# Masked attention with a rational FFN on one core: the planner's DMA reckoning, fillers for TensorE, and the products with V in two steps

## The chip, the cores and the metric

The kernel runs on one core of a Trainium2 chip. The core has four engines that compute (PE, the matrix engine, with its weight loads shown apart as PEld; DVE, the vector engine; ACT, the scalar engine; POOL) and SP, which here only issues DMAs. Each engine works through its own list of instructions in the written order and waits on semaphores where an instruction needs another engine's result. The metric is device time in microseconds (us), lower is better.

## What is computed

Eight batches of eight heads, 576 positions, 64 values per head. The attention keeps only scores within tau of the row's maximum; the heads' outputs side by side are the rows x of a feed-forward network with a rational activation.

```python
def _attn_ref(q, k, v, tau) -> np.ndarray:
    scale = 1.0 / np.sqrt(q.shape[-1])
    scores = scale * np.matmul(q, k.transpose(0, 1, 3, 2))
    thresh = np.max(scores, axis=-1, keepdims=True) - tau
    scores = np.where(scores >= thresh, scores, -1000000000.0)
    scores = scores - np.max(scores, axis=-1, keepdims=True)
    attn = np.exp(scores)
    attn = attn / (np.sum(attn, axis=-1, keepdims=True) + 1e-09)
    return np.matmul(attn, v).astype(np.float32)
...
    h = x @ w_in
    h2 = h * h
    h3 = h2 * h
    P = a[0] + a[1] * h + a[2] * h2 + a[3] * h3
    Q = 1.0 + np.abs(b[0]) * np.abs(h) + np.abs(b[1]) * h2
    g = P / (Q + 1e-06)
    return (g @ w_out).astype(np.float32)
```

x has 4608 rows of 512, w_in is 512 x 2048, w_out 2048 x 512, all in float32.

## The kernel before

**Precision.** A float32 factor is carried as two float16 parts, a rounded part ("hi") and a remainder ("lo"), and a product of two such factors is three float16 products: hi by hi, lo by hi, hi by lo. This holds for both FFN products and, after the first batch, for probabilities times V. In the first batch (PLAIN) that product runs in float32 and the transposes are made by TensorE.

**Attention.** The work is cut into units: a pair of heads and a tile of 128 queries (four full tiles and a rest of 64). For a unit PE multiplies queries and keys (lines 915, 922, 926), DVE takes the row maxima (932), ACT applies threshold and exponential (947, 951) into a buffer e, ACT or DVE writes the rounded part to a buffer hi (through the helper at 381) and DVE the remainder back over e (973). SP then issues two transposing DMAs (983), pT from hi and pT from e, and for two units together PE multiplies with V (1044): 30 matmuls of a 64-column array tiling, two heads side by side, five chunks c of the keys, three products each. ACT and DVE copy the result to x as two parts (1054, 1060).

**FFN.** A step takes 256 rows of x and 8 blocks of w_in: PE (1289), then a chain of ACT and DVE operations on tiles t (1299 to 1354), then PE with w_out (1363). ACT or DVE scales the result (1371, 1377), and it is stored (1386, 1390).

**Loads.** The weights come first, on POOL's DMA queue, each 1 MB load waiting on an earlier one (565). Q and K (755 to 766) and V (799, 803) of a pair come when their buffers (two, two and five) are free; from the ninth pair on they are on POOL's queue, while transposes and the copies of V's rounded part (863) are on SP's. POOL also computes the FFN's gains (1171 to 1217).

**Who sets the order.** Nothing in it is left to run time. A planner (class Plan) holds every operation with its engine (or a choice of engines, FLEX), its assumed duration, its dependencies and the buffers and PSUM banks that it takes and drops, and a key, which is its due time: a position in the sequence of units plus a constant for its kind (K) plus a shift of its unit or FFN step (SHIFT_UNITS, SHIFT_STEPS). order() simulates the engines: again and again it takes the operation that can start first and, among those within a tolerance (TOL), the one with the lowest key; the code is then emitted in that order. A DMA is a further engine of this simulation, "DMA" for SP's queue and "GD" for POOL's: it holds its queue for its duration, and its result counts as there a fixed LAT later (2.5 us on SP's queue, 3.3 on POOL's), no matter what else is under way. A transpose is given TPD, 1.3 us. Up to 120 us of planned time (LOADS_END) there are special rules: a load on POOL's queue is followed by a pause (PACED), a copy on SP's queue lasts twice as long plus 1 us, and a load on it lands 2 us later (LATE). A change of the array's tiling costs PE some 0.1 us in the plan (TURN), but doesn't enter the choice between operations while LAM is 0. Where PE has a pause in the plan, f_warm puts matmuls of an identity by itself into a free bank (1527) for 60% of the pause, before 400 us alone:

```python
            if e == "PE" and self.warm is not None and t < WARM_END:
                n = int((t - free[e]) * WARM / 0.22)
```

PSUM has eight banks. Scores of the first SINGLE units use either of two sets of three (0 to 2, 3 to 5), those of later units 0 to 2 alone; sums over w_out use one of 3 to 5, the first FFN product one of 5 and 6 (BH), and products with V, transposes on PE and small sums one of 7, 6 and 5 (B1).

Of the kernel before, what the change touches and what calls it, by code (L numbers as in the profile page):

```python
# [32 lines left out]
ENDK, ENDS = 2.59, 37.189  # L33

WHEN = [(-0.4, 1.998), (4.745, 1.263), (9.569, -0.366), (13.179, -0.311)]

V0, V1 = -1.222, -6.236

SINGLE = 22
# [35 lines left out]
AHEAD_RANK = 3.164  # L75

AHEAD = (1,) * 5 + (2,) * 11
PACED = (3.4, 0.5)
# [11 lines left out]
K = {"f1": 2.538, "f2": -0.829, "f4": -0.987, "f6": -1.195, "load": -5.828, "junk": 1.648, "sq": 1.739, "cn": -3.045,  # L90
     "cs": 0.032, "s1": -0.568, "s2": -5.401, "wh": 4.797, "wl": 1.319, "wc": 0.864, "vl": 0.529, "vc": 1.068, "vh": 1.802,
     "qk": -0.548, "max": -1.889, "thr": -0.221, "pre": -1.075, "sum": 2.999, "rec": 1.092, "rec2": 0.121, "diag": -0.725,
# [4 lines left out]

SHIFT_STEPS = {0: -0.894, 1: 3.213, 2: 0.769, 3: 3.605, 4: 1.271, 5: -0.037, 6: 1.022, 7: -0.168, 8: -1.488, 9: 2.739, 10: 0.4,
# [3 lines left out]

SHIFT_UNITS = {0: -1.177, 1: -0.45, 2: -1.342, 3: -1.061, 4: -1.427, 5: -0.333, 6: -0.175, 7: -0.27, 8: -2.113, 9: 0.228,
# [17 lines left out]

SHIFT_OPS = {}

LAM = 0.0

START = {"ACT": 4.777, "DVE": 4.281}
START_END = 104.113
EARLY = {"ACT": 1.482, "DVE": 4.089}
EARLY_END = 2093.721
PRICE = {"ACT": 10.914, "DVE": 0.624}  # L130

TOL = {"PE": 0.224, "ACT": 0.001, "DVE": 0.109, "POOL": 0.1, "DMA": 0, "GD": 0}
WARM, WARM_END = 0.6, 400.0

LOADS_END = 120.0

# [26 lines left out]
class Plan:  # L163
# [39 lines left out]
    def paced(self, e, o, t):  # L203
        if e != "GD" or not o.take or t >= LOADS_END:
            return 0.0
# [1364 lines left out]
```

## Time and profile before

| what | value |
|---|---|
| device time, median of 3 runs | 1319.86 us (1318.55 to 1327.18) |
| the profiled execution's own time | 1316.94 us |
| its span, first to last instruction | 1315.2 us |
| mean granted clock of TensorE | 0.979 |
| chain that ended last, by engine | PE 23%, ACT 14%, DVE 14%, DMA 8%, issue 4% |
| longest line of that chain | PE L1363 9%, DMA pT<-e 8%, PE L1289 6% |

How to read the rows: an instruction is named by its line (L1044), its engine, its operation, and what it writes and reads (pT<-e: the transpose that writes pT from e). "x30" counts instructions. Times behind an arrow are idle time of the engine, and the name behind the arrow is what ended it. A wait's row has the total in us, the number of waits and the longest. SPq and POOLq are the sequencers that issue DMAs. The granted clock is the share of TensorE's full clock.

### The profile page before, as it was taken

To read this page: it belongs to the slowest core of one execution; us is meant where nothing else is said; L and a number is where in the kernel's file an instruction comes from. 1 tells how busy PE (TensorE), PEld (TensorE's weight loads), DVE (VectorE), ACT (ScalarE), POOL (GpSimd) and SP (SyncE) were. 2 spreads that over 40 slices of the span, in tenths; PEclk is the share of its full clock that TensorE was granted. 3 is DMA by queue.
4 is the path that set the end of the run, shared out by engine and by line. 5 is a ranking of instruction groups with operands and counts; after the bars stand their busy time and mean duration, and the time that the engine had idled before them with its cause. 6 is when DMAs were issued, how large, how long until landed. Compare 5 with 4: busy or idle time off the path is not lost.

```text
span 1315.2 us, 25492 instructions
## 1 busy us (share of the span) xinstructions
PE 1222.9 (93%) x9444; PEld 786.3 (60%) x9444; DVE 1191.3 (91%) x1697; ACT 1142.1 (87%) x2165; POOL 392.3 (30%) x678
## 2 busy tenths in 40 slices
PE   7888899999998889999999799999999999999996
PEld 5556666675664646656656466675656665675652
DVE  6999999999997979999999689999989989999766
ACT  6999999998997979999998689999989888995643
POOL 2220240423142511552046241352315353400121
PEclk9999999999998989999999899999999999999998
DMA  8572285678557675586555684677547557650200
GB/s 226 201 236 84 87 156 98 120 163 171 92 116 115 136 109 102 105 163 130 92 113 96 103 160 97 136 147 150 90 88 151 122 133 140 123 97 18 53 16 16
DMA packets 344172, 156.30 MB, mean 119 GB/s; under 512 B 315136, under 2 KB 325104, under 8 KB 344048
## 3 DMA queue, kind: packets, MB, share of 16 engines
q1 hardware_dynamic: 321424, 93.83, 39.7%
q0 software_dynamic: 22304, 60.25, 17.0%
q8 instruction: 75, 1.23, 0.4%
q10 hardware_dynamic: 320, 0.59, 0.2%
q14 instruction: 49, 0.40, 0.1%
HBM read 63.25 MB, written 9.44 MB: 55 GB/s over the span
## 4 chain that ended last, share of the span: by engine, by line
PE 23%; ACT 14%; DVE 14%; DMA 8%; issue 4%; POOL 2%; POOLq 0%; ACTq 0%; DVEq 0%
PE banks L1363 9%; DMA pT<-e 8%; PE banks L1289 6%; PE banks L1044 4%; ACT e L947 3%; PE banks L926 3%; ACT e L951 2%; DVE e L973 2%; ACT hi L381 2%; DVE st L932 2%; DVE t L1354 2%; DVE t L1318 1%; ACT t L381 1%; DVE t L1328 1%; ACT t L1321 1%
## 5 line engine op out<-in xcount | busy, mean ns | idle before, releaser
L1363 PE MATMUL banks<-wp,t 128*128 128x512 f16 x1728 | 404.7, 383 | 11.1 <-ACT t L381 6.4
L1289 PEld LDWEIGHTS <-wi 128*128 128x128 f16 x3456 | 332.6, 98 | 97.6 <-issue 45.9
L1289 PE MATMUL banks<-x,wi 128*128 128x256 f16 x3072 | 364.1, 274 | 2.7 <-ACT t L1299 2.4
L1363 PEld LDWEIGHTS <-t 128*128 128x128 f16 x1728 | 164.0, 99 | 225.9 <-issue 45.6
L947 ACT ACTIVATE e<-banks,st 128x576 f32<-128x576 f32 x288 | 210.1, 740 | 27.2 <-DMA pT<-e 15.5
L951 ACT ACTIVATE e<-e,cf 128x576 f32<-128x576 f32 x288 | 223.1, 781 | 0.1
L973 DVE SCALAR_TENSOR_TENSOR e<-e,st,hi 128x576 f16<-128x576 f32 x252 | 201.9, 810 | 8.8 <-ACT hi L381 7.7
L932 DVE TENSOR_REDUCE st<-banks 128x2 f32<-128x1152 f32 x128 | 172.7, 1349 | 19.9 <-PE banks L926 14.2
L381 ACT ACTIVATE hi<-e,st 128x576 f16<-128x576 f32 x220 | 168.5, 774 | 5.6 <-DVE st L962 3.3
L1044 PE MATMUL banks<-pT,V 128*64 128x256 f16 (+1 forms) x2520 | 129.3, 254 | 35.8 <-DMA pT<-e 24.6
L1044 PEld LDWEIGHTS <-V 128*64 128x64 f16 x2520 | 107.7, 113 | 69.4 <-issue 50.8
L926 PE MATMUL banks<-KK,QQ 64*128 64x512 f32 x512 | 146.9, 651 | 0.0
L1299 ACT ACTIVATE t<-banks,hsc 128x512 f32<-128x512 f32 (+1 forms) x192 | 109.9, 586 | 21.0 <-PE banks L1289 17.4
L755 POOL DMA_DIRECT2D QQ<-in_qT_dram x47 | 25.2, 536 | 341.2 <-PE banks L915 193.1
L1354 DVE SCALAR_TENSOR_TENSOR t<-t,gsc,t 128x1024 f16<-128x1024 f32 (+2 forms) x69 | 90.7, 1323 | 12.0 <-ACT t L381 11.8
L1321 ACT ACTIVATE t<-t,co 128x1024 f32<-128x1024 f32 (+2 forms) x69 | 82.0, 1188 | 19.4 <-DVE t L1328 12.5
L1332 DVE SCALAR_TENSOR_TENSOR t<-t,co,t 128x1024 f32<-128x1024 f32 (+2 forms) x69 | 91.3, 1323 | 7.0 <-ACT t L1324 6.8
L1314 DVE SCALAR_TENSOR_TENSOR t<-t,co 128x1024 f32<-128x1024 f32 (+2 forms) x69 | 91.3, 1323 | 6.1 <-ACT t L1299 6.1
L381 ACT ACTIVATE t<-t,gsc 128x1024 f16<-128x1024 f32 (+1 forms) x66 | 78.1, 1197 | 18.2 <-DVE t L1340 12.7
L1340 DVE SCALAR_TENSOR_TENSOR t<-t,co,t 128x1024 f32<-128x1024 f32 (+2 forms) x69 | 91.2, 1322 | 0.1
L1328 DVE SCALAR_TENSOR_TENSOR t<-t,co,t 128x1024 f32<-128x1024 f32 (+2 forms) x69 | 91.2, 1322 | 0.0
L1318 DVE SCALAR_TENSOR_TENSOR t<-t,co 128x1024 f32<-128x1024 f32 (+2 forms) x69 | 91.1, 1322 | 0.0
(184 smaller groups left out, 1666.3 us busy)
## 6 DMA issues: line engine op xcount, KB each, us to landing
KK<-in_kT_dram POOLq DMA_DIRECT2D x94, 144.0 KB, 3.5
t<-in_w_in_dram POOLq DMA_DIRECT2D x8, 1024.0 KB, 7.2
t<-in_w_out_dram POOLq DMA_DIRECT2D x8, 1024.0 KB, 5.8
QQ<-in_qT_dram POOLq DMA_DIRECT2D x47, 144.0 KB, 3.0
V<-in_v_dram POOLq DMA_DIRECT2D x24, 256.0 KB, 4.0
out_dram<-u POOLq DMA_DIRECT2D x24, 256.0 KB, 3.8
QQ<-in_qT_dram POOLq DMA_DIRECT2D x47, 128.0 KB, 3.9
V<-u SPq DMA_DIRECT2D x28, 160.0 KB, 2.5
```

Of the source, the lines that this page charges most:

```text
L381: nc.scalar.activation(dst, src, AF.Identity, scale=factor)
L926: nc.tensor.matmul(d, QQ[r, t * P:(t + 1) * P], KK[r, REM:S], **one)
L932: nc.vector.tensor_reduce(box["st"][:, 0:2], box["both"], AX.X, ALU.max, negate=True)
L947: nc.scalar.activation(ev(hh), box["s"][hh], AF.Prelu, scale=SCALE, bias=box["st"][:, 2 + hh:3 + hh], alpha=STEEP)
L951: nc.scalar.activation(e, e, AF.Exp, scale=passes, accum_out=box["st"][:, 4 + hh:5 + hh])
L973: nc.vector.scalar_tensor_tensor(box["lo"][:, c], ev(hh), box["st"][:, 6 + hh:7 + hh], box["hi"][:, c], ALU.mult, ALU.subtract)
L1044: nc.tensor.matmul(dst, V[:, c * P + head * D:c * P + (head + 1) * D], rhs, start=c == 0 and n == 0, stop=c == NT and n == 2)
L1289: nc.tensor.matmul(d, wi_tile(c, f0 + j, hl), x[:, c, :], start=c == 0 and n == 0, stop=c == NC - 1 and n == 2)
L1299: nc.scalar.activation(box["h3"][:, 2 * k:2 * k + 2, sl], psv[:, :, sl], AF.Identity, scale=hsc[:, b2, g:g + 1])
L1328: nc.vector.scalar_tensor_tensor(r, r, a1, cols("h", x), ALU.add, ALU.mult)
L1354: nc.vector.scalar_tensor_tensor(gl, cols("r", x), gscale, gh, ALU.mult, ALU.subtract)
L1363: nc.tensor.matmul(acc[tt], g[x][:, o:o + P], wo_tile(f, y), start=begins and j == n == 0, stop=ends and j == nb - 1 and n == 2)
```

## The change

No tile, buffer size or table of engine choices is altered, and the matmuls with V remain the same 2520. What changes:

1. Each DMA carries an amount of queue time (move, 0.4 to 3.45 us; negative marks a transpose). The plan keeps one running time for the DMAs of SP's queue and one for those of POOL's; where the two overlap, each is lengthened by the share in SHARE, and an operation's result counts as there when its queue's time has passed it plus LANDS. The durations that a DMA holds its issuing engine are shorter for some (0.95 for 3.0 us for a weight load). The special rules up to 120 us go; a weight load instead waits in the plan for the landing of the one that the code makes it wait for.
2. WARM_END goes from 400 us to 1e9: pauses of PE in the plan are filled in the whole run.
3. The product with V (f_av) is emitted in two steps under two operations. The first has 20 matmuls: rounded and remainder part of V with the rounded probabilities. The second has 10: rounded V with the remainders. The first depends on the transposes of hi, the second on those of e. Both use the same bank, which is freed after the copies of x, as before.
4. Claims in the plan: in the first batch pT is claimed by PE's transpose rather than by the copy after it, and of an FFN step's pieces the later ones follow the first, which claims the tiles.
5. LAM becomes 2.353, so a change of tiling counts against an operation in the choice; the tolerances, the prices of a choice of engine (START, EARLY, PRICE), and all keys and shifts have new values. One unit fewer uses the first set of score banks (SINGLE).

The tables K, SHIFT_STEPS and SHIFT_UNITS, all of whose values are new, are left out below; K gains an entry for the second step (avl).

```diff
-ENDK, ENDS = 2.59, 37.189
+ENDK, ENDS = 3.881, 37.35
...
-SINGLE = 22
+SINGLE = 21
...
-PACED = (3.4, 0.5)
...
-LAM = 0.0
...
-TOL = {"PE": 0.224, "ACT": 0.001, "DVE": 0.109, "POOL": 0.1, "DMA": 0, "GD": 0}
-WARM, WARM_END = 0.6, 400.0
-LOADS_END = 120.0
-LATE = 2.0
+LAM = 2.353
...
+TOL = {"PE": 0.063, "ACT": 0.0, "DVE": 0.082, "POOL": 0.1, "DMA": 0, "GD": 0}
+WARM, WARM_END = 0.6, 1e9
+SHARE, SET_OUT, LANDS = (1.47, 0.75), 1.22, (0.53, 0.93)
...
     def pe(self, tiling, *args):
         o = self.op("PE", *args)
         o.tiling = tiling
+        return o
+
+    def move(self, work, *args):
+        o = self.op(*args)
+        o.work = work
         return o
...
-
-    def paced(self, e, o, t):
-        if e != "GD" or not o.take or t >= LOADS_END:
-            return 0.0
-        self.loads += 1
-        return PACED[AHEAD[min(self.loads, len(AHEAD) - 1)] - 1]
...
                     if t is not None:
+                        if o.paced and len(self.loads) >= AHEAD[len(self.loads)]:
+                            t = max(t, self.loads[-AHEAD[len(self.loads)]] + 0.1)
                         if e == "PE":
                             t = max(t, free[e] + TURN.get((tiling, o.tiling[0]), 0.0))
                         starts.append((t, o))
...
-            if e == "DMA" and o.drop and t < LOADS_END:
-
-                o.dur = 2.0 * o.dur + 1.0
             free[e] = end = t + o.dur
             busy[e] += o.dur
             if e in ("POOL", "GD"):
-                free["POOL"] = free["GD"] = end + self.paced(e, o, t)
+                free["POOL"] = free["GD"] = end
             if e == "PE":
                 tiling = o.tiling[1]
-            late = LATE if e == "DMA" and not o.drop and t < LOADS_END else 0.0
-            seen = end + self.LAT[e]
+            seen, landed = end + self.LAT[e], None
+            if o.work:
+                c = int(e == "GD")
+                moved[c] = max(moved[c], t + SET_OUT)
+                both = min(abs(o.work), max(0.0, moved[1 - c] - moved[c]))
+                moved[c] += abs(o.work) + SHARE[0] * both
+                moved[1 - c] += SHARE[1] * both
+                seen = landed = moved[c] + LANDS[o.work > 0]
+                if o.paced:
+                    self.loads.append(landed)
...
-                    d.ready[x] = max(d.ready[x], end + late + (self.OWN[e] if x == e else self.TO.get((e, x), self.LAT[e])))
+                    d.ready[x] = max(d.ready[x], landed if landed is not None and x != e else
+                                     end + (self.OWN[e] if x == e else self.TO.get((e, x), self.LAT[e])))
...
-        l = op("GD", 3.0, key - 2.0 + K["load"], ld, (), [hold])
+        l = plan.move(3.45, "GD", 0.95, key - 2.0 + K["load"], ld, (), [hold])
+        l.paced = True
...
-        q_done[bp] = [op(eng, 1.6 if eng == "GD" else 1.9, p0, ldq, (), [qh])]
+        q_done[bp] = [plan.move(1.43, eng, 1.6 if eng == "GD" else 1.9, p0, ldq, (), [qh])]
...
-        k_done[bp] = [op(eng, 0.1 if begin else 1.1 + 1.1 * (NT in ts) + 0.2 * (eng == "DMA"), p0 + 0.1, ldk, (), [kh])]
+        k_done[bp] = [plan.move(1.26 + 0.44 * (NT in ts), eng, 0.1 if begin else 1.1 + 1.1 * (NT in ts) + 0.2 * (eng == "DMA"), p0 + 0.1, ldk, (), [kh])]
...
-            v_done[bp] = op("DMA", 0.8, p + K["vc"], vc, [o], (), [vhi])
+            v_done[bp] = plan.move(0.68, "DMA", 0.5, p + K["vc"], vc, [o], (), [vhi])
...
-            l = v_loaded[bp] = op(eng, 1.9, max(q, V0 + V1 * pr, -5.0 + 0.1 * pr), ld, (), [vhold])
+            l = v_loaded[bp] = plan.move(1.43, eng, 1.9, max(q, V0 + V1 * pr, -5.0 + 0.1 * pr), ld, (), [vhold])
...
-        two = pairs.setdefault((bp, t // 2), {"pT": Hold("pT", 1), "tp": []})
+        two = pairs.setdefault((bp, t // 2), {"pT": Hold("pT", 1 if is_plain(bp, t) else 2), "tp": [], "low": []})
...
-        def f_av():
+        def f_av(steps):
             pT = place(two["pT"])
             VL, VH = (v_part(vh_[bp].slot, i) for i in range(2))
-            box["av"] = bank(bhs["av"])[:, 0:w2]
-            for c in range(NT + 1):
-                for n, (V, lo) in enumerate(((VH, 0), (VH, 1), (VL, 0))):
+            if 0 in steps:
+                box["av"] = bank(bhs["av"])[:, 0:w2]
+            for n in steps:
+                V, lo = ((VH, 0), (VL, 0), (VH, 1))[n]
+                for c in range(NT + 1):
                     for hh in range(2):
                         head = 1 - hh if full else hh
                         pp = slice(head * D, (head + 1) * D)
...
-                tr = plan.pe("ff" if piece < 2 else "cc", 0.92 if piece < 2 else 0.32, p + K["tr"], lambda x=piece, h=hold: f_tr(x, h), [dg], [hold],
-                        [e_hold, dg_hold])
-                take = [two["pT"]] if not two["tp"] and t % 2 == 0 else ()
+                tr = plan.pe("ff" if piece < 2 else "cc", 0.92 if piece < 2 else 0.32, p + K["tr"], lambda x=piece, h=hold: f_tr(x, h),
+                             [dg, two.get("tr")], [hold] + ([two["pT"]] if not two["tp"] and t % 2 == 0 else []), [e_hold, dg_hold])
+                two.setdefault("tr", tr)
                 two["tp"].append(op(FLEX["ev" if piece < 2 else "ev1"], 0, p + K["ev"], lambda x=piece, h=hold: f_ev(x, h),
-                                    [tr] + two["tp"][:1], take, [hold]))
+                                    [tr], (), [hold]))
         else:
...
-            tp = op("DMA", TPD if full else 0.6 * TPD, p + K["tph"], lambda: f_tp("hi"), his + two["tp"], [two["pT"]] if t % 2 == 0 else (),
+            tp = plan.move(-1.54 if full else -0.86, "DMA", TPD if full else 0.6 * TPD, p + K["tph"], lambda: f_tp("hi"), his + two["low"], [two["pT"]] if t % 2 == 0 else (),
                     [hi_hold])
-            tp = op("DMA", TPD if full else 0.6 * TPD, p + K["tpl"], lambda: f_tp("lo"), los + [tp], (), [e_hold])
             two["tp"].append(tp)
+            tp = plan.move(-1.54 if full else -0.86, "DMA", TPD if full else 0.6 * TPD, p + K["tpl"], lambda: f_tp("lo"), los + [tp], (), [e_hold])
+            two["low"].append(tp)
...
-            av = plan.pe("cc", 1.64 if full else 0.5, p + K["av"], f_av, two["tp"] + [v_low(bp), x_first.get(ck)], [bh] + first, [two["pT"], vh_[bp]])
+            av = plan.pe("cc", 1.09 if full else 0.33, p + K["av"], lambda: f_av((0, 1)), two["tp"] + [v_low(bp), x_first.get(ck)], [bh] + first, [two["pT"]])
+            av = plan.pe("cc", 0.55 if full else 0.17, p + K["avl"], lambda: f_av((2,)), two["low"] + [av], (), [two["pT"], vh_[bp]])
...
-            A = op(can(act(0.094), dve(0.068, 1.92)), 0, p + K["A"], on(f_A), [h], [hq] if t0 else ())
-            r2 = op("DVE", dve(0.128), p + K["r2"], on(f_r2), [h], [hr] if t0 else ())
+            A = op(can(act(0.094), dve(0.068, 1.92)), 0, p + K["A"], on(f_A), [h, holds.get("q")], [hq] if t0 else ())
+            r2 = op("DVE", dve(0.128), p + K["r2"], on(f_r2), [h, holds.get("r")], [hr] if t0 else ())
+            holds.setdefault("q", A)
+            holds.setdefault("r", r2)
...
-                    op("DMA" if late else "GD", 0.6 if kind == "m" else 1.1, p + K["st"], lambda tt=tt: f_st(tt), [o], (), [ho])
+                    plan.move(1.0 if kind == "m" else 1.16, "DMA" if late else "GD", 0.6 if kind == "m" else 1.1, p + K["st"], lambda tt=tt: f_st(tt), [o], (), [ho])
```

More of the change, by code (lines that the diff above doesn't have):

```diff
@@ L32 @@
 LEAD, SPACE0, SPACING = 4.456, 6.048, 3.976
-ENDK, ENDS = 2.59, 37.189
-WHEN = [(-0.4, 1.998), (4.745, 1.263), (9.569, -0.366), (13.179, -0.311)]
-V0, V1 = -1.222, -6.236
-SINGLE = 22
+ENDK, ENDS = 3.881, 37.35
+WHEN = [(-0.4, 1.998), (4.745, 1.263), (9.571, -0.366), (13.138, -0.311)]
+V0, V1 = -2.68, -9.448
+SINGLE = 21
 VISITED = 8
@@ L73 @@
 TPD = 1.3
-AHEAD_RANK = 3.164
+AHEAD_RANK = 3.199
 AHEAD = (1,) * 5 + (2,) * 11
-PACED = (3.4, 0.5)
 RECENT = 30.0
@@ L88 @@
         "wh": {"ACT": 1.05, "DVE": 0.662}, "twice": {"ACT": 0.135, "DVE": 0.085}}
-K = {"f1": 2.538, "f2": -0.829, "f4": -0.987, "f6": -1.195, "load": -5.828, "junk": 1.648, "sq": 1.739, "cn": -3.045,
-     "cs": 0.032, "s1": -0.568, "s2": -5.401, "wh": 4.797, "wl": 1.319, "wc": 0.864, "vl": 0.529, "vc": 1.068, "vh": 1.802,
-     "qk": -0.548, "max": -1.889, "thr": -0.221, "pre": -1.075, "sum": 2.999, "rec": 1.092, "rec2": 0.121, "diag": -0.725,
[4 rows of a table removed]
-SHIFT_STEPS = {0: -0.894, 1: 3.213, 2: 0.769, 3: 3.605, 4: 1.271, 5: -0.037, 6: 1.022, 7: -0.168, 8: -1.488, 9: 2.739, 10: 0.4,
[3 rows of a table removed]
-SHIFT_UNITS = {0: -1.177, 1: -0.45, 2: -1.342, 3: -1.061, 4: -1.427, 5: -0.333, 6: -0.175, 7: -0.27, 8: -2.113, 9: 0.228,
[17 rows of a table removed]
-SHIFT_OPS = {}
-LAM = 0.0
[L126 to L130, printed above, removed]
-TOL = {"PE": 0.224, "ACT": 0.001, "DVE": 0.109, "POOL": 0.1, "DMA": 0, "GD": 0}
-WARM, WARM_END = 0.6, 400.0
-LOADS_END = 120.0
-LATE = 2.0
+K = {"f1": 2.879, "f2": -0.977, "f4": -1.642, "f6": -2.297, "load": -13.257, "junk": -0.639, "sq": 0.511, "cn": -7.063,
+     "cs": -0.574, "s1": -0.84, "s2": -1.793, "wh": 5.727, "wl": -0.073, "wc": -1.225, "vl": 0.902, "vc": 7.288, "vh": 3.401,
+     "qk": -0.335, "max": -2.169, "thr": -0.202, "pre": -0.504, "sum": 2.684, "rec": 1.207, "rec2": -0.419, "diag": -2.928,
[4 rows of a table added]
+SHIFT_STEPS = {0: -1.408, 1: 5.147, 2: -1.564, 3: 1.158, 4: 0.21, 5: -0.954, 6: 1.452, 7: 1.558, 8: -0.529, 9: 2.6, 10: -0.347,
[3 rows of a table added]
+SHIFT_UNITS = {0: 0.203, 1: 1.416, 2: 0.6, 3: -0.378, 4: 0.358, 5: 0.055, 6: -2.766, 7: -0.535, 8: -5.864, 9: -0.653, 10: -0.836,
[17 rows of a table added]
+SHIFT_OPS = {}
+LAM = 2.353
+START = {"ACT": 5.233, "DVE": 3.75}
+START_END = 86.531
+EARLY = {"ACT": 1.726, "DVE": 4.382}
+EARLY_END = 2556.068
+PRICE = {"ACT": 10.42, "DVE": 8.917}
+TOL = {"PE": 0.063, "ACT": 0.0, "DVE": 0.082, "POOL": 0.1, "DMA": 0, "GD": 0}
+WARM, WARM_END = 0.6, 1e9
+SHARE, SET_OUT, LANDS = (1.47, 0.75), 1.22, (0.53, 0.93)
 TURN = {("h", "r"): 0.095, ("f", "r"): 0.095, ("h", "c"): 0.092, ("f", "c"): 0.17, ("r", "h"): 0.112, ("r", "f"): 0.21,
@@ L151, in __init__ @@
         self.wait = 0
+        self.work, self.paced = 0.0, False
         self.ready = dict.fromkeys(engs, 0.0)
@@ L176, in __init__ @@
         self.rank = self.shift = 0.0
-        self.loads = 0
+        self.loads = []
     def pe(self, tiling, *args):
@@ L240, in order @@
         done, busy = [], dict.fromkeys(engines, 0.0)
+        moved = [0.0, 0.0]
         left = len(self.ops)
@@ L444, in masked_attention_rational_ffn @@
     WS = 512
-    co = op("DMA", 1.2, 4.0, load_coefficients)
+    co = plan.move(0.4, "DMA", 1.2, 4.0, load_coefficients)
     co = op("ACT", 0.22, 6.0, lambda: nc.scalar.activation(cv[:, 0:2], cf[:, 4:6], AF.Abs), [co])
@@ L697, in masked_attention_rational_ffn @@
             o = op(FLEX["s2"], 0, k0 + K["wl"], f_wl, [o])
-            wo_done += [op("DMA", 1.0, k0 + K["wc"], f_wc, [o], (), [hu])] * 2
+            wo_done += [plan.move(1.0, "DMA", 0.6, k0 + K["wc"], f_wc, [o], (), [hu])] * 2
     half, rest = list(range(NT // 2)), [NT]
@@ L771, in load_ops @@
             keys = ldk
-            k = v_loaded[bp] = op(eng, 3.2 + 1.2 * (NT in ts), p0 + 0.1, lambda: (keys(), ld()), (), [kh, vhold])
+            k = v_loaded[bp] = plan.move(3.0, eng, 3.2 + 1.2 * (NT in ts), p0 + 0.1, lambda: (keys(), ld()), (), [kh, vhold])
             k_done[bp] = [k]
@@ L1410, in moe_ops @@
             hk.append(h)
-        piece_of, gl_of = {}, {}
+        piece_of, gl_of, holds = {}, {}, {}
         p1 = p
```

48 rows, old and new, of tables (K, SHIFT_STEPS, SHIFT_UNITS) are left out of this document.

## The prediction

> **What bounds the kernel now.** I read the page's busy shares first, then the stretches, then the waits, then the chain inside the worst stretches.
>
> ```profile
> span 1315.2 us, 25492 instructions
> PE 1222.9 (93%) x9444; PEld 786.3 (60%) x9444; DVE 1191.3 (91%) x1697; ACT 1142.1 (87%) x2165; POOL 392.3 (30%) x678
> ```
>
> Three engines lie within 81 us of each other, so no single one is the bound; whatever stops one of them soon stops the others. Next the stretches (columns: span; busy us of PE, its weight loads, DVE, ACT, POOL; granted clock; DMA share; GB/s).
>
> ```profile
> 0.00:150.00 150.00, 126.17 (x880) 88.46 (x882) 129.83 (x287) 134.79 (x250) 25.78 (x62) 0.97 0.56 179
> 150.00:1200.00 1050.00, 996.98 (x7955) 639.60 (x7956) 978.49 (x1343) 953.11 (x1856) 348.03 (x599) 0.98 0.63 120
> 1200.00:1315.20 115.20, 99.75 (x613) 58.25 (x611) 83.00 (x69) 54.16 (x62) 18.49 (x19) 0.97 0.11 29
> 350.00:400.00 50.00, 48.59 (x418) 32.26 (x417) 48.79 (x68) 48.51 (x94) 23.03 (x38) 1.00 0.61 122
> 400.00:450.00 50.00, 42.27 (x326) 24.57 (x324) 41.79 (x56) 40.05 (x82) 15.45 (x30) 0.93 0.73 124
> 450.00:500.00 50.00, 43.55 (x325) 28.50 (x326) 41.91 (x58) 41.51 (x77) 10.59 (x19) 0.93 0.60 106
> 500.00:550.00 50.00, 48.46 (x371) 30.78 (x369) 48.81 (x62) 48.63 (x94) 19.04 (x30) 1.00 0.52 106
> 700.00:750.00 50.00, 40.44 (x340) 26.82 (x340) 36.52 (x49) 37.53 (x83) 23.84 (x37) 0.90 0.63 102
> 750.00:800.00 50.00, 47.10 (x398) 32.70 (x397) 44.87 (x67) 44.76 (x87) 20.48 (x37) 0.97 0.71 136
> 950.00:1000.00 50.00, 45.79 (x326) 27.80 (x325) 43.81 (x55) 44.08 (x84) 13.63 (x23) 0.97 0.53 104
> 1050.00:1100.00 50.00, 46.88 (x440) 29.23 (x436) 43.66 (x62) 42.38 (x87) 23.58 (x37) 0.97 0.63 131
> 1100.00:1150.00 50.00, 47.80 (x366) 31.48 (x363) 46.44 (x70) 47.08 (x93) 23.30 (x37) 0.97 0.73 136
> ```
>
> A good stretch (350 to 400, 500 to 550) keeps PE and DVE above 48 of 50. I measure a bad one by DVE, which has no granted clock to blur the count: against 48.8 the stretches 400:450, 450:500 and 700:750 lack 7.0 + 6.9 + 12.3 = 26.2 us, and 750:800, 950:1000, 1050:1100 and 1100:1150 lack 3.9 + 5.0 + 5.1 + 2.4 = 16.4. Together 42.6 us: what a better order could fetch between 150 and 1200. The waits say what stops the engines there.
>
> ```profile
> PE banks L1044 <- DMA pT<-e: 24.6, 17, 3.8
> ACT e L947 <- DMA pT<-e: 15.5, 12, 5.0
> PE banks L922 <- ACT e L947: 14.8, 15, 4.5
> PE banks L1044 <- DMA pT<-hi: 9.3, 5, 5.1
> DMA to landing us min/median/max: 2.6/3.4/11.5
> ```
>
> PE waits 24.6 + 9.3 = 33.9 us at the products with V (L1044) for transposed probabilities, and 14.8 more at the scores (L922) behind ACT, which for 15.5 us had no free e buffer because a transpose had not yet read it. That is 48.7 of the 53.0 us (1050.0 - 997.0) that PE idles in the middle. The last row is the transposes' own: 3.4 us from issue to landing in the median, 11.5 at worst. The timeline of one bad place shows why:
>
> ```profile
> 717.71 0.79 POOL L799 DMA_DIRECT2D V<-in_v_dram  x1
> 719.43 2.92 SPq L983 DMA_TRANSPOSE pT<-e  x1
> 720.24 0.52 POOL L762 DMA_DIRECT2D KK<-in_kT_dram  x1
> 720.75 0.52 POOL L763 DMA_DIRECT2D KK<-in_kT_dram  x1
> 727.67 0.42 PE L1044 MATMUL banks<-pT,V 128*64 128x256 f16 x2 [5.08 <-DMA pT<-hi]
> 731.01 3.20 PE L1044 MATMUL banks<-pT,V 128*64 128x256 f16 x28 [2.91 <-DMA pT<-e]
> 719.43 11.54 DMA pT<-e
> ```
>
> Loads of V and KK are issued around the transposes, these land late (the last row is the chain of waits: 11.54 us on that one), and PE stands twice, first for the rounded part (pT from hi), then, two matmuls later, for the remainder (pT from e). The old planner charges a transpose 1.3 us and 2.5 us to landing, whatever the loads do.
>
> **The change, part by part.** The sum is made against the profiled execution: 1316.94 us, a span of 1315.2 and 1.74 around it. It stands 2.92 below the median, 1319.86.
>
> *Shared queues (move, SHARE, SET_OUT, LANDS; LOADS_END, PACED and LATE go).* No instruction is added: every load, copy, store and transpose keeps its form, and only the order on each engine shifts, through the planned landings. I count this part, the retuned keys (K, SHIFT_STEPS, SHIFT_UNITS, LAM, TOL, one unit less under SINGLE, the earlier claim on pT and the waits of later pieces on the first) as one term. A transpose that the plan knows to be late gets other products ahead of its consumer. The upper end is all 42.6 us; the lower is nothing, since PE is already 95% busy there (997.0 of 1050) and a filled pause must take its work from elsewhere. I take two thirds of the three big places (17), where the plan was furthest out, and half of the other four (8): -25. If that cover is not there, the price is the 33.9 us of waits as they stand. POOL's loads still wait for buffers, and still come in bunches, so the next late thing is the load itself (QQ, KK) for the scores.
>
> *Two steps for the products with V.* Before, c is the outer loop: after the two matmuls of the first c with hi, the next two need lo. Now 20 of 30 matmuls (VH and VL with hi) run once the rounded parts landed, and a second step of 10 follows when the remainders have. The matmuls keep their number and shape. What is bought is part of the 24.6 us above, and I count it in the -25, not again. The price is two more changes of the array's tiling wherever other work parts the steps. From an undisturbed place:
>
> ```profile
> 818.03 0.83 PE L1289 MATMUL banks<-x,wi 128*128 128x256 f16 x6
> 818.78 1.83 PE L1044 MATMUL banks<-pT,V 128*64 128x256 f16 x30
> 820.54 1.70 PE L1289 MATMUL banks<-x,wi 128*128 128x256 f16 x14
> L1289 PE MATMUL banks<-x,wi 128*128 128x256 f16 x3072 | 364.1, 274 | 2.7 <-ACT t L1299 2.4 <-DVE xr L1060 0.2
> L1044 PE MATMUL banks<-pT,V 128*64 128x256 f16 (+1 forms) x2520 | 129.3, 254 | 35.8 <-DMA pT<-e 24.6 <-DMA pT<-hi 9.3 <-DVE xr L1060 1.5
> L983 SPq DMA_TRANSPOSE pT<-hi x140: 1200/1302/2417, 163.0 to 1230.7; - x140
> ```
>
> The 2520 of the row for L1044 make 84 products of 30, which run two at a time. The 14 of L1289 start every (1.70 - 0.274) / 13 = 0.11 us, so six are through at 818.03 + 0.66 = 818.69 and the product starts 0.09 later. The product's 15 pairs at the same 0.11 end at 820.43, and L1289 starts 0.11 later. A parted product costs 0.20 us; 84 of them 16.8 at most, 0 if none is parted. Remainders land after the rounded parts by at least one transpose on the same queue (1.3 us of its issue time each, last row), longer than 10 pairs of matmuls take (1.1), so I take three quarters, 63 x 0.20 = 12.6 us of PE. Half of it falls in PE's remaining pauses: +6 on the path, 0 to 16.8 as ends. The wait added is PE's for the remainder, ahead of the second step: behind it stands all later PE work in the written order, and ACT's copy of x (L1054) waits for it as it did before.
>
> *Pauses filled over the whole run (WARM_END 400 to 1e9).*
>
> ```profile
> 0.00:175.00 175.00, 20.16 (x124) 17.20 (x124) 0.97 0.54 165
> 175.00:400.00 225.00, 0.77 (x4) 0.68 (x4) 1.00 0.67 131
> 400.00:1315.20 915.20, 0.00 (x0) 0.00 (x0) 0.98 0.56 107
> 1289.22 22.08 PE banks L1363 x95
> 470.85 4.71 PE L1363 MATMUL banks<-wp,t 128*128 128x512 f16 x21
> L1363 PE MATMUL banks<-wp,t 128*128 128x512 f16 x1728 | 404.7, 383 | 11.1 <-ACT t L381 6.4 <-DVE t L1354 4.6
> ```
>
> The first three rows are the fillers alone (L1527). They go where the plan has a pause, not where the chip has one: once the pipeline runs, 4 in 225 us. At that rate the other 915 us get 16, at 20.9 / 128 = 0.16 us each 2.6 us; with an order that plans later landings I allow 100, or 16 us if none lay in a real pause. What they could save is the clock after a pause, granted at 0.90 to 0.93 in the three bad stretches and at 1.00 in the good ones. The 95 matmuls of the last chain took 22.08 us; at (4.71 - 0.38) / 20 = 0.22 us each they need 20.6, so a warm start of the tail is worth 1.5. The same loss after the three big stalls is already inside the DVE count. I take -1 for the tail and +1 for fillers that lie in no pause: 0, from -3 to +16.
>
> *Begin and end.* The first 150 us lose the artificial pauses behind weight loads in the plan; on the chip those loads still wait for the one before. ACT, the busiest engine there, has 134.8 of 150, so a better order could find some of 15 us and a worse one lose as much; I allow two fifths of it, 6, either way. In the last 115 us DVE and ACT wait along one chain that is not cut differently. I take 0 for both, -6 to +6.
>
> Sum: -25 + 6 + 0 + 0 = -19. 1316.94 - 19 = 1297.9 for a profiled execution, and with the 2.92 of the median 1300.9, forecast 1301. Its own range is 1290 to 1311.
>
> **Rivals.**
> *The order takes nearly all of it.* If all 42.6 come back and the turns lie in pauses: 1319.9 - 42.6 = 1277.3, some 1278. For it: 48.7 of 53.0 us of idle PE name the transposes. Against: DVE and PE would both have to run at the pace of the best stretches throughout.
> *The reckoning doesn't bite.* Loads start when buffers come free, transposes when DVE is done, both on the chip's own clock, so a planned landing may be as wrong as before; then the turns eat what small gain there is: -6 + 6, 1320. For it: POOL's loads wait for PE, so a small slip moves a whole bunch. Against: the late places are few and large, and they sit where loads and transposes were issued together.
> *Turns that cost a whole matmul.* If each change of tiling waits until the matmul in flight is through (0.27 us by the mean of L1289, not the 0.09 to 0.11 read above), 63 parted products cost 63 x 2 x 0.27 = 34 us of PE, half of it on the path: 1319.9 - 25 + 17 = 1312. For it: the steps are parted just where PE is full. Against: the two turns measured above, both undisturbed. The Trainium skill, TensorEngine Tiling (Array Packing), section Key Properties, states this rule: changing the tiling mode drains TensorE; this trace shows a cost of that kind, but only some 0.1 us of it.
> *Slower: the split product sits on its bank.* The bank of a product (7, 6 or 5) is now taken when the rounded part has landed and freed only after the remainder; the first FFN product (L1289) uses 5 and 6 too. Held through a median landing, each blocked one costs up to 3.4 us on PE. At 19 / 3.4 = 6 blocked products of 84 the gain is gone; at (19 + 13.2) / 3.4 = 10 it is 1% slower, at 12 the time is 1342. For it: three engines at 87% and more leave nothing to absorb it. Against: L1289 waits only 2.7 us now, as the row above shows, and the planner knows the banks.
>
> **How the numbers follow.** One per cent, 13.2 us, is about what a measurement can tell from no change. Forecast 0.52 (most of it past 1%: 0.45 faster, 0.07 same), nearly all 0.17 (faster), doesn't bite 0.15 (0.02 faster, 0.11 same, 0.02 slower), whole-matmul turns 0.06 (same), bank 0.10 (0.02 same, 0.08 slower). Faster 0.64, same 0.26, slower 0.10. The range runs from the second case to just past the third, 1278 to 1322, and takes in the fourth: it leaves out the bank case (0.10) and about half of the largest gain (0.08).
>
> **What would show it.** Right: PE's idle before the products with V falls from 33.9 to under 15 us, even with both steps counted; the stretches with a clock of 0.90 to 0.93 are gone from the middle; a timeline shows runs of 20 and of 10 matmuls with other work between; under 100 fillers after 400 us. Wrong: the idle time moves to L1289 (banks), to L922 (e buffers) or to loads of QQ and KK; PE's busy time grows by over 13 us from turns and fillers; transposes still land 10 us late with PE standing beside them.

## The result and the profile after

The changed kernel takes 1269.33 us (median of 4 runs, 1267.42 to 1272.44); the ratio to the kernel before is 0.9597, 95% interval 0.9553 to 0.9641. That is 4.0%, some 54 us of the 1323.07 of the kernel before in the same comparison (4 runs), where 19 were forecast, and it lies 9 us under the lower end of the range. Between the two profiled executions it is 44.5 us (1316.94 and 1272.44). The same program timed once more, in a later comparison (start_fill below), took 0.9656 of the kernel before, so the gain is 3.4 to 4.0%. One later run of the kernel before, 1542.32 us at a granted clock of 0.748, is a slow execution and enters no ratio. Lines after 30 are shifted in the changed kernel: products with V are L1053 (before L1044), the FFN's products L1300 and L1374 (L1289, L1363), scores L922, L929 and L933 (L915, L922, L926), the exponential's first pass L954 (L947), fillers L1540 (L1527).

The page's head and the stretches of the changed kernel (columns as before: span; busy us of PE, weight loads, DVE, ACT, POOL; granted clock; DMA share; GB/s):

```profile
span 1270.4 us, 25729 instructions
PE 1212.7 (95%) x9537; PEld 799.3 (63%) x9542; DVE 1193.7 (94%) x1701; ACT 1132.5 (89%) x2163; POOL 387.8 (31%) x678
```

```profile
0.00:150.00 150.00, 124.60 (x803) 86.82 (x808) 125.58 (x275) 125.48 (x233) 22.19 (x55) 0.90 0.52 166
150.00:1200.00 1050.00, 1024.94 (x8355) 674.61 (x8352) 1021.37 (x1387) 978.82 (x1903) 363.06 (x614) 1.00 0.64 124
1200.00:1270.40 70.40, 63.15 (x386) 37.90 (x383) 46.73 (x41) 28.25 (x29) 2.55 (x9) 0.99 0.04 15
50.00:100.00 50.00, 37.60 (x192) 25.20 (x194) 42.01 (x76) 42.77 (x75) 8.98 (x14) 0.76 0.49 165
```

The row from 150 to 1200 carries the result. DVE does 1021.4 us of work there instead of 978.5: 42.9 us more, so the whole of the 42.6 that the good stretches left as a ceiling was fetched, not 25. The granted clock is 1.00 instead of 0.98. In DVE's idle time, the span's 44.8 us are 42.9 less from 150 to 1200, 8.5 less after 1200 (32.2 to 23.7), 4.2 more before 150, and 2.4 us more of work. What is left after 1200 us is 70 us instead of 115, because the work was done earlier. The first 150 us became worse: DVE does 4 us and ACT 9 us less in them, at a clock of 0.76 from 50 to 100.

In PE's terms the span shrank by 44.8: idle time from 92.3 to 57.7 us, busy time from 1222.9 to 1212.7, although fillers grew from 20.9 to 33.8 us. PE's own work thus takes 23 us less with the same matmuls. The two FFN products alone have 16 of them (404.7 and 364.1 us before), near the 15 that a rise of the granted clock from 0.98 to 1.00 would give (an estimate, 2% of their 768.8):

```profile
L1374 PE MATMUL banks<-wp,t 128*128 128x512 f16 x1728 | 393.8, 379 | 4.5 <-DVE t L1365 4.4
L1300 PE MATMUL banks<-x,wi 128*128 128x256 f16 x3072 | 358.8, 273 | 6.9 <-ACT t L1310 6.2 <-DVE x L1069 0.4
```

The waits of the changed kernel, and the transposes' time to landing:

```profile
PE banks L929 <- ACT e L954: 10.8, 11, 4.9
PE banks L1300 <- ACT t L1310: 6.2, 6, 3.1
PE banks L1053 <- DMA pT<-hi: 2.5, 5, 0.9
PE banks L1053 <- DMA pT<-e: 2.0, 3, 1.2
ACT e L954 <- DMA pT<-e: 1.5, 2, 1.3
```

```profile
DMA to landing us min/median/max: 2.5/3.4/10.3
```

PE waits 4.5 us for transposes at the products with V instead of 33.9, ACT 1.5 for an e buffer instead of 15.5 and 2.4 for a hi buffer instead of 1.1. Together that is 8.4 us instead of 50.5. The wait at the scores behind ACT fell less, from 14.8 to 10.8, so part of it had another cause than the late transposes that the prediction read there. But the transposes are as late as ever: 3.4 us in the median and 10.3 at worst, against 3.4 and 11.5. What changed is what the engines have in front of them meanwhile. One such place in the timeline of the changed kernel:

```profile
312.56 2.09 SPq L990 DMA_TRANSPOSE pT<-hi  x1
314.74 2.01 SPq L990 DMA_TRANSPOSE pT<-e  x1
315.10 0.52 POOL L762 DMA_DIRECT2D QQ<-in_qT_dram  x1 [0.59 <-PE banks L933]
315.36 4.70 PE L1374 MATMUL banks<-wp,t 128*128 128x512 f16 x21
316.97 0.52 POOL L769 DMA_DIRECT2D KK<-in_kT_dram  x1
319.43 1.98 SPq L990 DMA_TRANSPOSE pT<-hi  x1
321.93 4.10 PE L1300 MATMUL banks<-x,wi 128*128 128x256 f16 x36
326.62 1.83 PE L1053 MATMUL banks<-pT,V 128*64 128x256 f16 x30 [0.59 <-DMA V<-u]
338.57 1.28 PE L1053 MATMUL banks<-pT,V 128*64 128x256 f16 x20
339.79 0.39 PE L1300 MATMUL banks<-x,wi 128*128 128x256 f16 x2
```

Transposes and loads are again issued together, and it is here that the 10.3 us occur (the transpose of 314.74 lands at 325.06), but 21 and 36 FFN matmuls stand ahead of the product, and it starts 0.59 us late, and for another reason. By then the remainders have landed too, so both steps run as one stretch of 30; at 338.57 the first step of the next pair runs alone.

### The profile page after: what moved, and what is told of

It reads as the page before. It is cut to its first block, busy times and chain, and to the rows that moved or that the text cites. A ratio compares the mean times of both kernels' runs of the same rounds, so it can differ in the third digit from the quotient of the medians.

```text
span 1270.4 us, 25729 instructions
## 1 busy us (share of the span) xinstructions
PE 1212.7 (95%) x9537; PEld 799.3 (63%) x9542; DVE 1193.7 (94%) x1701; ACT 1132.5 (89%) x2163; POOL 387.8 (31%) x678
## 4 chain that ended last, share of the span: by engine, by line
PE 28%; DVE 17%; ACT 10%; DMA 4%; issue 4%; POOL 3%; DVEq 0%; ACTq 0%; POOLq 0%; SPq 0%
PE banks L1374 14%; PE banks L1300 8%; DVE e L980 3%; DVE st L939 3%; PE banks L933 2%; PE banks L1053 2%; ACT e L958 2%; ACT e L954 2%; DMA pT<-e 2%; DVE t L1339 2%; DVE t L1351 2%; DVE t L1329 1%; ACT hi L387 1%; DVE t L1365 1%; DMA pT<-hi 1%
## 5 line engine op out<-in xcount | busy, mean ns | idle before, releaser
L1374 PE MATMUL banks<-wp,t 128*128 128x512 f16 x1728 | 393.8, 379 | 4.5 <-DVE t L1365 4.4
L1300 PEld LDWEIGHTS <-wi 128*128 128x128 f16 x3456 | 333.5, 98 | 81.0 <-issue 32.3
L1300 PE MATMUL banks<-x,wi 128*128 128x256 f16 x3072 | 358.8, 273 | 6.9 <-ACT t L1310 6.2
L1374 PEld LDWEIGHTS <-t 128*128 128x128 f16 x1728 | 164.6, 98 | 204.4 <-issue 20.6
L954 ACT ACTIVATE e<-banks,st 128x576 f32<-128x576 f32 x288 | 210.8, 740 | 10.6 <-DVE st L948 8.3
L387 ACT ACTIVATE hi<-e,st 128x576 f16<-128x576 f32 x214 | 164.8, 773 | 5.0 <-DMA pT<-hi 2.4
L933 PE MATMUL banks<-KK,QQ 64*128 64x512 f32 x512 | 147.4, 653 | 0.0
L1053 PEld LDWEIGHTS <-V 128*64 128x64 f16 x2520 | 103.4, 110 | 57.9 <-issue 51.0
L1053 PE MATMUL banks<-pT,V 128*64 128x256 f16 (+1 forms) x2520 | 121.0, 248 | 7.2 <-DMA pT<-hi 2.5
L1347 DVE SCALAR_TENSOR_TENSOR t<-t,t 128x1024 f32<-128x1024 f32 (+2 forms) x69 | 87.1, 1262 | 0.2
```

What stands on the lines that cost most here:

```text
L387: nc.scalar.activation(dst, src, AF.Identity, scale=factor)
L933: nc.tensor.matmul(d, QQ[r, t * P:(t + 1) * P], KK[r, REM:S], **one)
L954: nc.scalar.activation(ev(hh), box["s"][hh], AF.Prelu, scale=SCALE, bias=box["st"][:, 2 + hh:3 + hh], alpha=STEEP)
L1053: nc.tensor.matmul(dst, V[:, c * P + head * D:c * P + (head + 1) * D], rhs, start=c == 0 and n == 0, stop=c == NT and n == 2)
L1300: nc.tensor.matmul(d, wi_tile(c, f0 + j, hl), x[:, c, :], start=c == 0 and n == 0, stop=c == NC - 1 and n == 2)
L1374: nc.tensor.matmul(acc[tt], g[x][:, o:o + P], wo_tile(f, y), start=begins and j == n == 0, stop=ends and j == nb - 1 and n == 2)
```

## The experiments

**Which part carries it?** Four kernels first. In "joined" and "fill_400" the planner writes the order of the changed kernel, in "before_inner" that of the kernel before, operation by operation (fill_400 without the later fillers). The kernel before was timed again beside each group: 1320.44 us in this one, 1314.53 in the second, 1318.7 in the last. Across groups the ratios say more than the microseconds.

joined: all 30 matmuls where the second step stood.

```diff
-            av = plan.pe("cc", 1.09 if full else 0.33, p + K["av"], lambda: f_av((0, 1)), ...
+            av = plan.pe("cc", 1.09 if full else 0.33, p + K["av"], lambda: None, ...
-            av = plan.pe("cc", 0.55 if full else 0.17, p + K["avl"], lambda: f_av((2,)), ...
+            av = plan.pe("cc", 0.55 if full else 0.17, p + K["avl"], lambda: f_av((0, 1, 2)), ...
```

> The changed kernel's order, but all 30 matmuls of a product with V stand where the second step stood (remainders landed); nothing else moves. If the order is what gained and the two steps are a detail (my theory): within 8 us of the changed kernel's 1269, since only 11 stretches of 20 and 11 of 10 matmuls stand alone in its trace. If the two steps carry the gain (rival): 25 us or more slower, 1294 up.

Measured 1276.61 us (1274.85 to 1278.15), ratio to before 0.966 (0.9619 to 0.97): 7 us slower than the changed kernel. The runs of the two don't overlap, the intervals of their ratios just do. Against the second timing of the changed kernel (1272.01 us, ratio 0.9656, start_fill below) it is 5 us, and nothing by the ratios. In the new order the two steps are worth little, 7 us at most.

before_inner: in the kernel before, the remainders last inside each product.

```diff
-            for c in range(NT + 1):
-                for n, (V, lo) in enumerate(((VH, 0), (VH, 1), (VL, 0))):
+            for n, (V, lo) in enumerate(((VH, 0), (VL, 0), (VH, 1))):
+                for c in range(NT + 1):
```

> The kernel before with its own order; only inside a product with V the ten matmuls with the remainders come last, so the 20 others run while the remainders are still on the way. Theory (order): the 17 waits for the remainder shrink by at most 1.1 us each, 5 to 15 us faster than 1323. Rival (two steps carry the gain): 25 us faster or more, 1298 down.

Measured 1299.84 us (1294.42 to 1302.95), ratio 0.9832 (0.9785 to 0.9878): 20 us faster, more than I expected and less than the rival asked. Its waits:

```profile
PE banks L922 <- ACT e L947: 12.6, 14, 3.0
PE banks L1044 <- DMA pT<-e: 11.3, 12, 2.6
PE banks L1044 <- DMA pT<-hi: 4.9, 4, 1.8
```

The products' 33.9 us fell to 16.2, 18 us less, about what was gained. The same idea is worth 20 us in an order that runs into the transposes and at most 7 in one that keeps clear of them.

fill_400: fillers up to 400 us of planned time alone.

```diff
-WARM, WARM_END = 0.6, 1e9
+WARM, WARM_END = 0.6, 400.0
```

> The changed kernel in the same order, fillers only up to 400 us of planned time. Theory (order): 1266 to 1273, since 126 fillers after 400 us are some 19 us of TensorE in real pauses. Rival (the fill over the whole run keeps the clock up): stretches of half clock come back in the middle and it is 8 to 20 us slower. Third way: the fillers cost, and it is 5 us or more faster.

Measured 1274.85 us (1273.49 to 1276.39), ratio 0.9647 (0.9608 to 0.9687): 5.5 slower than the changed kernel, again with intervals that overlap, outside my 1273 and short of the rival's 8. Against the second timing (1272.01, ratio 0.9656) it is 2.8, so the time alone settles little. The traces show a difference at the end; the last stretch of fill_400 with its last chain of matmuls, and then those of the changed kernel:

```profile
1240.00:1273.60 33.60, 23.92 (x96) 9.96 (x96) 17.28 (x20) 8.72 (x11) 0.00 (x0) 0.83 0.04 16
1246.41 23.31 PE L1374 MATMUL banks<-wp,t 128*128 128x512 f16 x95 [3.66 <-DVE t L1365]
```

```profile
1240.00:1270.40 30.40, 23.79 (x122) 11.95 (x121) 16.98 (x20) 8.20 (x10) 0.00 (x0) 0.98 0.05 17
1245.89 20.68 PE L1374 MATMUL banks<-wp,t 128*128 128x512 f16 x95 [2.78 <-DVE t L1365]
```

Without the fillers the tail's clock is 0.83, its last 95 matmuls take 2.6 us more, and it is 3.2 us longer in all.

after_jit1: every entry of K, SHIFT_STEPS and SHIFT_UNITS moved at random.

```diff
+    r = random.Random(seed)
+    for d in (K, SHIFT_STEPS, SHIFT_UNITS):
+        for k in d:
+            d[k] += r.uniform(-by, by)
...
+_jitter(1, 0.1)
```

> The changed kernel with every key and shift moved by a random amount of at most 0.1 of a unit, so the same parts in a slightly other order. If the new reckoning of landings gains by itself, with any sensible keys: 1265 to 1285. If the gain lies in keys fitted to it one by one: 1295 to 1320, most of the gain gone.

Measured 1303.17 us, ratio 0.9845 (0.9789 to 0.9901). So over half of the gain hangs on keys fitted to the planner, and the reckoning doesn't gain with just any keys. This is one draw of random keys. The table below shows where the time goes: the planner's own end is 30 us later with them, and the chip keeps that plan almost as well as the changed kernel's.

**The reckoning, or the keys?** Four more.

before_inner_fill: before_inner with WARM_END at 1e9.

```diff
-WARM, WARM_END = 0.6, 400.0
+WARM, WARM_END = 0.6, 1e9
```

> The kernel before, its own order, with the remainders last inside each product and fillers over the whole run: the two parts of the change that need no new order. The first alone gave 1300. If the order with its reckoning of landings is what is left of the gain (theory): 1288 to 1300, no nearer to 1269. If the two mechanical parts make most of it together (rival): 1275 to 1285.

Measured 1298.6 us, ratio 0.9874 (0.9805 to 0.9943): in the old order the fillers add nothing that can be told from before_inner. From here to 1269, 29 us, the order makes the difference, with the parting of the steps in it.

new_code_old_keys: the changed code with the key tables, LAM, tolerances, prices and other tuned constants of the kernel before.

```diff
-LAM = 2.353
+LAM = 0.0
...
-TOL = {"PE": 0.063, "ACT": 0.0, "DVE": 0.082, "POOL": 0.1, "DMA": 0, "GD": 0}
+TOL = {"PE": 0.224, "ACT": 0.001, "DVE": 0.109, "POOL": 0.1, "DMA": 0, "GD": 0}
```

> The changed code (reckoning of landings, two steps, fillers) with all keys, shifts, tolerances and prices of the kernel before, LAM 0. Theory (reckoning and keys fitted to it go together; moving keys by 0.1 cost 34 us): 1300 to 1330, no better than the kernel before with the two mechanical parts. Rival (the reckoning gains with any sensible keys): 1275 to 1295.

Measured 1355.52 us, ratio 1.0288 (1.0233 to 1.0343): slower than the kernel before, and slower than I expected. Its plan is already 53 us longer than that of the kernel before (1290.9 and 1238.2, table below), and its waits show the products with V stopped by transposes again:

```profile
PE banks L1053 <- DMA pT<-e: 17.9, 17, 2.9
PE banks L1053 <- DMA pT<-hi: 12.6, 17, 2.5
```

no_share: the keys of the changed kernel, loads and transposes blind to each other.

```diff
-SHARE, SET_OUT, LANDS = (1.47, 0.75), 1.22, (0.53, 0.93)
+SHARE, SET_OUT, LANDS = (0.0, 0.0), 1.22, (0.53, 0.93)
```

> The changed kernel with SHARE at zero: each queue keeps its own landings, but loads and transposes no longer lengthen each other in the plan; keys as fitted with sharing. By the theory that sharing is what the plan must know: slower than the changed kernel with keys moved at random (1303), 1305 to 1330, with transposes in the waits of PE again. Rival (any disturbance of the order costs the same): 1295 to 1305, with the waits spread as in that run.

Measured 1316.75 us, ratio 0.9984 (0.995 to 1.0018): the whole gain is gone. By ratio it is slower than with keys moved at random (0.9845), which speaks for sharing. The other sign failed: waits of PE and ACT that a transpose ended are 27.1 us here and 33.1 in after_jit1. And the keys don't fit this planner, so it doesn't settle it.

start_fill: 36 fillers asked for ahead of the twelfth unit's scores, in the first 150 us.

```diff
+                if o.fn.__name__ == "f_qk":
+                    self.scores += 1
+                    n = max(n, EXTRA.get(self.scores, 0))
...
+EXTRA = {12: 36}
```

> The changed kernel, same order, with 36 fillers more ahead of the twelfth unit's scores, where TensorE waits 4.85 us at 63 to 68 us and then runs at half clock to 84. If the half clock after that wait is what the first 150 us lost against the kernel before: 3 to 8 us faster, 1261 to 1266, and the half clock from 67 to 84 is gone. Rival (ACT and DVE limit there): within 2 us of 1269.

Measured 1272.01 us, ratio 0.9656 (0.9608 to 0.9705), no difference. It tells nothing about the clock: the planner puts fillers only into a free PSUM bank, had none at that place, and wrote the order of the changed kernel, operation for operation. So these four runs are the changed kernel's a second time, and the stretch stayed at a low clock, as its row shows:

```profile
70.00:100.00 30.00, 22.93 (x106) 15.90 (x106) 22.14 (x44) 23.68 (x40) 3.93 (x8) 0.66 0.51 180
```

**Both planners with keys fitted to them.** To part reckoning and fit, keys were fitted for both: a random search of about 7,300 steps over K, SHIFT_STEPS and SHIFT_UNITS (and a little over TOL, START and EARLY) that keeps what brings the planner's own end forward. It began from the moved keys of after_jit1 with sharing reckoned, and from those of the changed kernel with SHARE at zero, twice each. All four have the two steps and the fillers. Beyond the new tables the diff to the changed kernel is none for the first two, and for the others that of no_share.

```diff
-K = {"f1": 2.879, "f2": -0.977, "f4": -1.642, "f6": -2.297, "load": -13.257, "junk": -0.639, "sq": 0.511, "cn": -7.063,
...
+K = {"A": 3.664, "av": 0.218, "avl": -0.656, "avp": 7.941, "cn": -13.88, "cs":
...
```

> The changed kernel from the keys moved by up to 0.1, then fitted again by a random search of some 7,300 steps against the planner's own end, with sharing reckoned; the planner puts its end 11.4 us behind that of the changed kernel. Theory (a plan that knows the sharing is one the chip keeps): 1275 to 1287, most of the 34 us back. Rival (only chip-tuned keys are good): 1295 to 1305 as before the search.

> The same search with another seed; the planner's end is 10.9 us behind that of the changed kernel. Theory: 1275 to 1287, within 8 us of the first. Rival: 1295 to 1305.

> The same search and number of steps on the kernel whose planner has SHARE at zero; by its own planner it ends 5.6 us behind the changed kernel, so 5 to 6 us ahead of the two fitted with sharing. Theory (sharing is what makes the plan hold): in spite of that 8 to 25 us slower than those two, 1290 to 1305. Rival (any plan is as good once its keys are fitted): 3 to 9 us faster than those two, 1270 to 1282.

> As the one before, another seed; by its own planner it ends 2.2 us behind the changed kernel and 8.7 to 9.2 ahead of those fitted with sharing. Theory: 1287 to 1303, slower than both fitted with sharing. Rival: 1268 to 1279.

"Planner's end" below is what order() itself puts into plan.total for the order that it writes. It is no time of the chip; the span of the profile beside it is. The last column is the span less the planner's end.

| kernel | sharing reckoned | planner's end | span | device time, median | ratio to before (95%) | chip behind plan |
|---|---|---|---|---|---|---|
| before | no | 1238.2 | 1315.2 | 1318.7 (19 runs) | 1 | 77 |
| changed | yes | 1236.8 | 1270.4 | 1269.33 | 0.9597 (0.9553 to 0.9641) | 34 |
| moved_refit1 | yes | 1248.1 | 1284.3 | 1290.34 | 0.9774 (0.9729 to 0.9819) | 36 |
| moved_refit2 | yes | 1247.6 | 1277.9 | 1280.68 | 0.9712 (0.9666 to 0.9758) | 30 |
| no_share_refit1 | no | 1242.3 | 1309.1 | 1309.92 | 0.9923 (0.9887 to 0.9959) | 67 |
| no_share_refit2 | no | 1239.0 | 1315.5 | 1313.78 | 0.994 (0.9898 to 0.9983) | 77 |
| after_jit1 | yes | 1266.8 | 1302.8 | 1303.17 | 0.9845 (0.9789 to 0.9901) | 36 |
| no_share | no | 1263.0 | 1309.8 | 1316.75 | 0.9984 (0.995 to 1.0018) | 47 |
| new_code_old_keys | yes | 1290.9 | 1354.9 | 1355.52 | 1.0288 (1.0233 to 1.0343) | 64 |

The two planners fitted without sharing promise 5 to 9 us less than the two fitted with it and deliver 20 to 33 us more; the intervals of the ratios lie apart. This falls on the theory's side, though no_share_refit1 and 2 came out even slower than its 1303 to 1305, moved_refit1 just past its 1287, and the two fitted with sharing lie 10 us apart rather than 8. The waits of the second of each, with sharing and without:

```profile
ACT e L952 <- DMA pT<-e: 6.7, 7, 2.0
ACT hi L385 <- DMA pT<-hi: 6.6, 4, 3.7
PE banks L1051 <- DMA pT<-hi: 5.1, 3, 2.7
PE banks L1051 <- DMA pT<-e: 1.9, 4, 0.8
```

```profile
ACT e L953 <- DMA pT<-e: 20.6, 13, 3.9
ACT hi L386 <- DMA pT<-hi: 13.4, 9, 3.9
PE banks L1052 <- DMA pT<-hi: 8.0, 4, 3.5
PE banks L1052 <- DMA pT<-e: 3.3, 5, 1.6
```

Without sharing in the plan, ACT loses 34.0 us to buffers that late transposes still hold; with it, 13.3. With PE's waits it is 45.3 and 20.3, and in the first of each 46.1 and 20.5: the same difference in both pairs, from two searches on each side. The old and the new kernel promise the same end within 2 us, each by its own reckoning: the change did not find a shorter plan but one that the chip can keep.

## Why the prediction was wrong

*The order with its reckoning, -25.* The mechanism was right: waits for transposes were the lost time, and a plan that knows of the shared queues avoids most of them, as the fitted pairs show. The size failed at "two thirds of the three big places and half of the other four". The ceiling read from the good stretches (42.6 by DVE) was reached in full (42.9). That it came out so exactly is partly luck of the keys: moved_refit1 and moved_refit2, with the same reckoning, do 31.8 and 34.0 us more of DVE's work from 150 to 1200 than the kernel before, about three quarters of the ceiling. The rival "the order takes nearly all of it" with its 1278 was nearest; I gave it 0.17 on the argument that three engines could not run at the pace of the best stretches throughout. They do: DVE is 97% busy from 150 to 1200. The two steps were rightly counted inside this term; the remainders put last give 20 us by themselves in the old order, and the two steps at most 7 in the new.

*Turns, +6.* There was no such cost. I took three quarters of 84 products as parted; in the order that the planner writes, 21 are. Counted in the traces, stretches of products with V without other matmuls between went from 79 to 76, with 11 stretches of 20 and 11 of 10 alone, all stretches on PE from 798 to 733, fillers included, and changes of the array's tiling from 452 to 380. My reading is that remainders mostly landed before the order came to the product, and that a plan that weighs turns (LAM) groups its work; LAM was not tried alone. The price of one turn was not at fault; the number was. The rival of whole-matmul turns fails on that price: at 338.57 the 20 matmuls of a first step, ten pairs at 0.11, are through at 339.67, and L1300 starts 0.12 later, not 0.27.

*Fillers, 0.* fill_400 is 5.5 us slower than the first timing of the changed kernel and 2.8 slower than the second, so the range of -3 to +16 is not clearly left. The estimate for the tail's last chain was good: 20.6 us with a warm start, and it took 20.68 (22.08 before, 23.31 in fill_400). That is partly luck: with the same fillers and the same pause ahead of it, it took 22.36 in joined. Fillers did not cost PE time elsewhere: DVE does 1021.4 us of work from 150 to 1200 with them and 1020.2 without. After 400 us there are 124, over the 100 allowed for, half of them in the tail; the rows of the fillers alone in the changed kernel:

```profile
400.00:1150.00 750.00, 9.84 (x66) 8.29 (x66) 1.00 0.64 126
1150.00:1270.40 120.40, 6.91 (x58) 6.63 (x58) 0.99 0.19 39
```

*Begin, 0 with 6 either way.* It is a loss inside that margin: 4.2 us of DVE's work by 150 us. Up to 400 us it stays at 3 to 5; by 450 the changed kernel is 3.6 ahead (416.2 us of DVE's work against 412.6). Why the planner accepts this, and what a kernel without it would take, stays open; start_fill could not tell.

*End, 0.* This holds: in the last 70.4 us DVE idles 22.4 us before and 23.7 after. The 8.5 us less after 1200 lie ahead of that, in the kernel before's time from 1200 to 1245 us.

*The other rivals.* "The reckoning doesn't bite" is refuted by the fitted pairs. "The split product sits on its bank" too: L1300 waits 6.9 us instead of 3.4 for L1289 (2.7 and 0.7), far from the 19 us at which it would decide.

*What would show it.* Idle before the products with V under 15 us: 4.5, or 7.2 with all causes. No stretch at 0.90 to 0.93 in the middle: right. Runs of 20 and 10 with other work between: there, but the exception. Under 100 fillers after 400 us: missed, 124. Transposes still 10 us late with PE beside them: late, yes, but PE works.

The steps that failed are thus two: a share of the ceiling taken by feel (25 us where 42.9 came), and turns put at three quarters of the products where a quarter is parted (+6 where none were added). One thing remains unexplained: new_code_old_keys reckons with sharing and is still 64 us behind its plan, with 48.5 us of waits for transposes on PE and ACT. Its tolerances, prices and LAM differ too, and these were not taken apart. So knowing of the sharing is not enough by itself; in this case it took keys near those fitted to it.

## What to carry to other kernels

Where an order is written out ahead, compare the end it promises with the span: the gap is what its cost model doesn't know, and the wait that explains most of it is a good candidate for what to model next. Here, keys fitted to a planner without the sharing gave at most 0.8%, and the old keys did worse under the new planner than under their own: after a change of the model they had to be fitted again. When bounding such a change, take the pace of the undisturbed stretches as within reach, and not as a far end to be discounted by feel; here one set of keys reached it and two others three quarters of it.

## What was not expected of the hardware

Transposes are no faster in a kernel that hardly waits for them: 3.4 us in the median and 10.3 at worst with 4.5 us of PE waiting, against 3.4 and 11.5 with 33.9.

Fillers kept the clock up at the end, and not every time in full. In fill_400, the changed kernel without its later fillers, 96 matmuls after 1240 us went with a clock of 0.83; with 26 fillers more (x122) it was 0.98. Over all the traces, the last 95 matmuls take 22.1 to 23.3 us without fillers ahead of them (before, before_inner, fill_400). In the eleven with fillers they take 20.7 us in five and 22.4 in six, and those six have 3.4 us at half clock within 1.4 us of the first of the 95. What decides between the two stays open: the changed kernel (20.7) and joined (22.4) have the same 42 fillers there and the same pause of 2.78 us after them.
